# Linear attention, layer 1: keys summed with normalised rows over the tokens instead of with values, and another written order of its beginning

## The chip, the cores and the metric

One Trainium2 chip, one core. The metric is the device time of one execution in microseconds. Lower is better.

## The reference

Four layers run over x of 2048 tokens by 576 columns, bf16, in the order A, B, A, B:

```python
phi = lambda t: where(t > 0, t + 1, exp(t)) + 1e-6
def A(y, wqkv, wo):              # 32 heads of 18 columns
    q, k, v = split_heads(y @ wqkv)
    pq, pk = phi(q), phi(k)
    kv = einsum("bhsd,bhse->bhde", pk, v)      # sum over the tokens s
    z  = einsum("bhsd->bhd", pk)
    o  = einsum("bhqd,bhde->bhqe", pq, kv) / (einsum("bhqd,bhd->bhq", pq, z)[..., None] + 1e-6)
    return join_heads(o) @ wo
def B(y, w1, b1, w2, b2):        # 576 -> 4608 -> 576
    return gelu(y @ w1 + b1) @ w2 + b2
x = x + A(layernorm(x)); x = x + B(layernorm(x)); x = x + A(layernorm(x)); x = x + B(layernorm(x))
```

The layernorm has no weights, and both A layers use the same `wqkv` and `wo`, both B layers the same MLP weights. Since v = y @ wv, the sum over tokens of pk and v can be done in two ways: make v for each token and sum pk with v, or sum pk with y and multiply that sum by wv once.

## The kernel before

**Tiles.** The tokens are 16 tiles of 128 (t = 0 to 15). The 576 columns are five row blocks of 128 (`KD`, the last holds 64), the heads five groups (`G`: four of seven heads, 126 columns, and one of four, 72). Keys are worked on in two halves of 288 columns (`HALF`). `yT` holds the turned (transposed) normalised rows of all tokens, `wqkv_sb` the weights of query, key and value (column parts 0, 1, 2).

**Entry and rows.** `load_x0` and `load_wqkv` issue the loads on SyncE in a written order (`chained`): rows of tiles 0 and 1, all key weights, rows of tile 2, value weights, rows 3 to 5, query weights, the other rows. `LNPipe` normalises rows stage by stage, one stage per `tick`: statistics on VectorE, the reciprocal root as a power on GpSimd (L374), the normalisation (L391 on GpSimd for tiles 2 and from 4 on, L395 on VectorE) from the row tile into one of three buffers `y_ring`, five transposes on TensorE (L423), and a copy into `yT` (tiles 0 and 1 halved between ScalarE and VectorE, L426 and L427, later ones on ScalarE, L430). The core's own engine queues run in program order; `add_manual_dep(..., NOSYNC)` fixes the order of two instructions on one engine. A call of `pe()` chains TensorE's instructions in the order of the text.

**Layer 1, first part.** For each tile: `k_proj` (L542: two halves of five matmuls, each through phi into `pk`), the layernorm's step of a later tile, `v_proj` (L560 and L563: ten matmuls of 252 and 324 columns, copied into `v_ring` with a column of ones), `kv_acc` of the tile before (L584: five matmuls that sum pk with v and, through the ones, z into one PSUM accumulator), and, from tile 4 on, one of the 20 query blocks `q_proj` (L590: 126 rows by 512 tokens). `phi_from_psum` makes phi from two ScalarE passes (exp L467, copy L468) and two VectorE operations (L475, L479); `phi_by_dve` from the exp (L453) and two VectorE operations (L454, L456), the last of which reads PSUM. Masks for heads are built on GpSimd by `masks(n)`, some steps at each tile; the weights for the later stages are loaded by `late_pieces`, one piece at each tile from tile 3 on.

**Layer 3, first part** (`li > 0`) has another form already. `k_half` (L614) makes one half of the keys of a tile; `rows_by_keys` (L631), three steps behind, sums that half with the five row blocks of the tile's normalised rows: chunk 4 (64 columns and one of ones) into `k2_tail` in a bank of the pool `ps_h`, chunks 0 to 3 into two pairs of banks (`ps_acc`). It goes over all tiles with half 0 and then with half 1. `kv_groups` (L651) multiplies the sums `k2` by the value weights, 5 matmuls for each group, and masks the heads; `kv_wo_half` (L669) multiplies by `wo`; z comes from the column of ones (L695).

**Second part of both layers**: denominators (`den_stage`, `quad_stage`), scaling of the queries, and `wo_stage` (L824), which adds the residual and hands tiles to the layernorm of the MLP. The MLP's first matmul is L953.

**PSUM.** Pool `ps_h` has four banks, taken in turn by everything with the tag `h` (key halves, transposes, query blocks and others); `ps_acc` holds two pairs.

Of the kernel before, what the change touches and what calls it, by code (L numbers as in the profile page):

```python
# [15 lines left out]
P = 128  # L16
# [18 lines left out]
def build(tc, A_x, A_wqkv, A_wo, B_w1, B_b1, B_w2, B_b2, out, dbg=None, n_layers=4):  # L35
    nc = tc.nc
    dbg = dbg or {}
    with ExitStack() as ctx:
# [14 lines left out]
        pow_warm = const.tile([P, 1], F32, name="pow_warm")  # L53
        nc.gpsimd.memset(pow_warm[:], 1.0)
        nc.gpsimd.tensor_tensor(out=pow_warm[:], in0=pow_warm[:], in1=neg_half[:], op=ALU.pow)
# [5 lines left out]
        z_row = const.tile([P, 1], BF16, name="z_row")  # L61
# [9 lines left out]
        def inner_diag(tile_, lead, n):  # L71
# [7 lines left out]
            select(maskz[:], 1.0, ALU.not_equal, -126, [[0, 7], [0, DH]], 1),  # L79
            fill(z_row, 0.0),  # L80
            select(z_row[:], 1.0, ALU.not_equal, -126, [[0, 1]], 1),
# [62 lines left out]

        def load_x0(t):
            x0 = blk.tile([P, D], BF16, name="x0", tag="blk")
            chained(nc.sync.dma_start(out=x0[:], in_=x_in[t * P:(t + 1) * P, :]))
            x0_tiles[t] = x0

        def load_wqkv(part):  # L150
            cols = slice(part * D, (part + 1) * D)
            chained(nc.sync.dma_start(out=wqkv_sb[:, 0:4, cols],
                                      in_=A_wqkv[0:4 * P, cols].rearrange("(k p) n -> p k n", p=P)))
            chained(nc.sync.dma_start(out=wqkv_sb[0:64, 4, cols], in_=A_wqkv[4 * P:D, cols]))
# [4 lines left out]
        load_wqkv(1)  # L159
        load_x0(2)  # L160
        load_wqkv(2)
        load_x0(3)
        load_x0(4)
        load_x0(5)
# [3 lines left out]
        for i in (NY - 1, 0, 1):  # L168
            nc.vector.memset(y_ring[i][:], 0.0)
# [8 lines left out]
        for vr in v_ring:  # L178
            nc.gpsimd.memset(vr[:, 4, 72:126], 0.0)
            nc.gpsimd.memset(vr[:, :, 126:127], 1.0)  # L180
            nc.gpsimd.memset(vr[:, :, 127:128], 0.0)
# [29 lines left out]
        def bias_casts():  # L211
# [3 lines left out]
        late_pieces = [(lambda i=i: piece_w1(i)) for i in range(9)] + [piece_wo] + \  # L215
                      [(lambda i=i: piece_w2(i)) for i in range(6)] + [piece_b1_dma]
# [16 lines left out]
        def tail_ones():  # L233
            for c in range(NCB):
                nc.gpsimd.memset(tails(c)[:, :, 64:65], 1.0)
# [65 lines left out]
        class LNPipe:  # L301
# [11 lines left out]
            def tick(self, transposes=1):  # L313
                land()
                for it in list(self.items):
# [32 lines left out]
                    elif st == 0:  # L348
# [10 lines left out]
                        if it["kind"] == "A" and it["t"] == 1 and it["load"] is None and it["evac"] == "act":  # L359
                            tc.add_manual_dep(aggr.ins, dve_last["norm"], NOSYNC, reason="first rows first")  # L360
                        if it["kind"] == "A" and it["t"] == 2 and it["load"] is None and it["evac"] == "act":
                            tc.add_manual_dep(aggr.ins, dve_last["turned"], NOSYNC, reason="first rows first")
# [7 lines left out]
                        it["mv"], it["u"] = mv, u  # L370
                        dve_last["u"] = var_eps.ins.name
                    elif st == 1:
                        rstd = work.tile([P, 1], F32, name="ln_rstd", bufs=6)
                        nc.gpsimd.tensor_tensor(out=rstd[:], in0=it["u"][:], in1=neg_half[:], op=ALU.pow)  # L374
                        it["rstd"] = rstd
                    elif st == 2 and it["norm"] != "dve":
# [3 lines left out]
                        it["nmr"] = nmr  # L380
                    elif st in (2, 3):
# [12 lines left out]
                        else:  # L394
                            norm = nc.vector.tensor_scalar(out=y[:, 0:D], in0=xt[:, 0:D], scalar1=it["mv"][:, 0:1],  # L395
                                                           scalar2=it["rstd"][:, 0:1], op0=ALU.subtract, op1=ALU.mult)
                            if it["kind"] == "A" and it["t"] == 1 and it["load"] is None and it["evac"] == "act":
                                tc.add_manual_dep(norm.ins, dve_last["turned"], NOSYNC, reason="first rows first")
# [9 lines left out]
                    elif st == 4:  # L408
                        y = it["y"]
                        t = it["t"]  # L410
                        if it["evac"] == "dma":
                            turn_rows(y, t, it["kind"])
                            self.items.remove(it)
                            continue
                        tp = ps_h.tile([P, 512], F32, name="tp", tag="h")
                        tp = tp[:, 0:DPAD // 2].bitcast(BF16).rearrange("p (k n) -> p k n", k=KD)
                        first = it["kind"] == "A" and t < 2
                        tp2 = tp
                        if first:
                            tp2 = ps_h.tile([P, 512], F32, name="tp2", tag="h")  # L420
                            tp2 = tp2[:, 0:DPAD // 2].bitcast(BF16).rearrange("p (k n) -> p k n", k=KD)
                        for k in range(KD):
                            pe(nc.tensor.transpose(out=(tp if k < 3 else tp2)[:, k, :], in_=y[:, k * P:(k + 1) * P],  # L423
                                                   identity=ident[:]))
                        if first:
                            act_last["turned"] = nc.scalar.copy(out=yT[:, 0:3, t * P:(t + 1) * P], in_=tp[:, 0:3, :]).ins.name  # L426
                            copy = nc.vector.tensor_copy(out=yT[:, 3:KD, t * P:(t + 1) * P], in_=tp2[:, 3:KD, :])  # L427
                            dve_last["turned"] = copy.ins.name
                        elif it["evac"] == "act":
                            turned_tile = nc.scalar.copy(out=yT[:, :, t * P:(t + 1) * P], in_=tp)  # L430
                            if act_last["exp"] is not None:
# [11 lines left out]
        phi0 = {}  # L443
# [7 lines left out]
        def phi_by_dve(ps_ap, out_ap, rows, n):  # L451
            e = work.tile([P, 512], BF16, name="phi_e", bufs=3)
            act_last["exp"] = nc.scalar.activation(out=e[0:rows, 0:n], in_=ps_ap, func=ACT.Exp).ins.name  # L453
            nc.vector.tensor_scalar(out=e[0:rows, 0:n], in0=e[0:rows, 0:n], scalar1=1.0, scalar2=1e-6,  # L454
                                    op0=ALU.min, op1=ALU.add)
            top = nc.vector.scalar_tensor_tensor(out=out_ap, in0=ps_ap, scalar=C1, in1=e[0:rows, 0:n],  # L456
                                                 op0=ALU.add, op1=ALU.max)
            dve_last["phi"] = top.ins.name

        def phi_from_psum(ps_ap, out_ap, rows, n, turned_cols=False, after=None, dve_after=None, ident_after=None,  # L460
                          exp_first=False):
# [10 lines left out]
            if ident_after is not None:  # L472
                tc.add_manual_dep(ident_pass.ins, ident_after, NOSYNC, reason="first rows first")
# [3 lines left out]
            if ident_after is not None:  # L477
                tc.add_manual_dep(low.ins, dve_last["turned"], NOSYNC, reason="first rows first")
# [3 lines left out]
            dve_last["phi"] = top.ins.name  # L482

# [46 lines left out]
        def layer_A(li, next_kind, pre_a1=None):  # L530
            kvacc_of = {}
            pk_tiles = {}
            v_tiles = {}
            pq = {}

            def k_proj(t):
                tok = slice(t * P, (t + 1) * P)
                pk = blk.tile([P, D], BF16, name="pk", tag="blk")
                for half in range(2):
                    kp = ps_h.tile([P, 512], F32, name="k_ps", tag="h")  # L540
                    for k in range(KD):
                        pe(nc.tensor.matmul(kp[:, 0:HALF], lhsT=yT[:, k, tok],  # L542
                                         rhs=wqkv_sb[:, k, D + half * HALF: D + (half + 1) * HALF],
                                         start=(k == 0), stop=(k == KD - 1)))
                    phi = phi_by_dve if half == 1 and (li > 0 or t < 2) else phi_from_psum
                    if li == 0 and t == 0 and half == 0:
                        lnp.tick()
                        phi_from_psum(kp[:, 0:HALF], pk[:, 0:HALF], P, HALF, ident_after=act_last["turned"])
                        continue
                    phi(kp[:, 0:HALF], pk[:, half * HALF:(half + 1) * HALF], P, HALF)  # L550
                pk_tiles[t] = pk

            def v_proj(t):
                tok = slice(t * P, (t + 1) * P)
                va = v_ring[state["vcnt"] % NV]
                state["vcnt"] += 1
                begin = li == 0 and t < 2
                vp = ps_acc.tile([P, 2, 512], F32, name="v_ps", tag="accA" if begin and t == 1 else "accB")
                for k in range(KD):
                    pe(nc.tensor.matmul(vp[:, 0, 0:252], lhsT=yT[:, k, tok], rhs=wqkv_sb[:, k, 2 * D: 2 * D + 252],  # L560
                                     start=(k == 0), stop=(k == KD - 1)))
                for k in range(KD):
                    pe(nc.tensor.matmul(vp[:, 1, 0:324], lhsT=yT[:, k, tok], rhs=wqkv_sb[:, k, 2 * D + 252: 3 * D],  # L563
                                     start=(k == 0), stop=(k == KD - 1)))
                copy = nc.scalar.copy(out=va[:, 0:4, 0:126].rearrange("p (b g) c -> p b g c", b=2),
                                      in_=vp[:, :, 0:252].rearrange("p b (g c) -> p b g c", g=2))
                if begin:
                    for keys in ("exp", "phi"):
                        tc.add_manual_dep(copy.ins, act_last[keys], NOSYNC, reason="keys before values")
                if begin and t == 1:  # L570
# [475 lines left out]
        def pre_a1_layer0(t):  # L1046
# [6 lines left out]
            if t >= 4:  # L1053
                masks(2)
# [75 lines left out]
```

## Time and profile before

| | |
|---|---|
| Median of 3 runs | 764.03 us (763.88 to 764.38) |
| Profiled execution | 763.95 us, span 762.2 us |
| TensorE clock granted | 1.00 throughout |
| TensorE matmul busy | 756.4 us, 99% (6594 matmuls) |
| ScalarE / VectorE / GpSimd busy | 336.2 (44%) / 270.1 (35%) / 126.3 (17%) us |
| First key matmul of layer 1 | 7.02 us |
| z sums of layer 1 | about 70.3 us |
| First MLP matmul of layer 2 | 104.62 us |
| z sums of layer 3 | about 444 us |

A row of the timeline reads: start and duration in us (of a run of instructions, from the first's start to the last's end), engine (PE is TensorE's matmul, PEld its weight load, DVE VectorE, ACT ScalarE, POOL GpSimd, SPq the queue of SyncE), line, operation, output <- inputs, shapes, count, and in brackets the idle time before it and what ended that. Runs of pipelined matmuls overlap in this view, so a run's own duration is longer than the step to the next run. The chain of waits gives start, duration, engine, tile and line for each piece of the chain that ended last. The table of windows gives a stretch, its length, and each engine's busy time with its instructions.

### The profile page before, as it was taken

To read this page: it belongs to the slowest core of one execution; us is meant where nothing else is said; L and a number is where in the kernel's file an instruction comes from. 1 tells how busy PE (TensorE), PEld (TensorE's weight loads), DVE (VectorE), ACT (ScalarE), POOL (GpSimd) and SP (SyncE) were. 2 spreads that over 40 slices of the span, in tenths; PEclk is the share of its full clock that TensorE was granted. 3 is DMA by queue.
4 is the path that set the end of the run, shared out by engine and by line. 5 is a ranking of instruction groups with operands and counts; after the bars stand their busy time and mean duration, and the time that the engine had idled before them with its cause. 6 is when DMAs were issued, how large, how long until landed. Compare 5 with 4: busy or idle time off the path is not lost.

```text
span 762.2 us, 15786 instructions
## 1 busy us (share of the span) xinstructions
PE 756.4 (99%) x6594; PEld 491.0 (64%) x6594; DVE 270.1 (35%) x684; ACT 336.2 (44%) x750; POOL 126.3 (17%) x198
## 2 busy tenths in 40 slices
PE   8999999999999999999999999999999999999998
PEld 5777664675477457646777767447645754674476
DVE  7786963136023503400355678600240032000000
ACT  5888857204610750264056577560164037205600
POOL 4681241002000301200110005300020021001000
PEclk9999999999999999999999999999999999999999
DMA  8993483016402621330246007530231033011000
GB/s 245 257 326 53 157 281 82 16 49 181 106 25 73 180 75 45 99 80 9 71 125 208 1 26 236 207 83 16 72 88 48 16 126 82 9 32 56 1 9 24
DMA packets 80289, 73.82 MB, mean 97 GB/s; under 512 B 36698, under 2 KB 64858, under 8 KB 80218
## 3 DMA queue, kind: packets, MB, share of 16 engines
q1 hardware_dynamic: 80218, 72.82, 32.8%
q8 instruction: 51, 0.84, 0.5%
q14 instruction: 20, 0.16, 0.1%
HBM read 48.03 MB, written 24.77 MB: 96 GB/s over the span
## 4 chain that ended last, share of the span: by engine, by line
PE 98%; DMA 1%; DVE 0%; SPq 0%; issue 0%
PE m_ps L1011 36%; PE h_ps L953 20%; PE hp_ps L953 16%; PE q_ps L590 6%; PE wo_ps L824 5%; PE k_ps L542 3%; PE k_ps L614 3%; PE k_ps L631 2%; PE v_ps L563 1%; PE m_half L1011 1%; PE v_ps L560 1%; PE tp L423 1%; DMA wqkv_sb<-in_A_wqkv_dram 1%; PE kvacc L584 1%; PE k_tail L631 1%; PE rden_ps L788 0%
## 5 line engine op out<-in xcount | busy, mean ns | idle before, releaser
L1011 PE MATMUL m_ps<-w_sb,hT 128*128 128x288 bf16 x2232 | 274.8, 286 | 0.0
L1011 PEld LDWEIGHTS <-hT 128*128 128x128 bf16 x2304 | 224.8, 98 | 59.8 <-issue 3.4
L953 PEld LDWEIGHTS <-w_sb 64*128 64x128 bf16 x2304 | 124.5, 94 | 136.5 <-issue 1.9
L953 PE MATMUL hp_ps<-yT,w_sb 64*128 64x512 bf16 x1152 | 178.0, 376 | 0.0
L953 PE MATMUL h_ps<-yT,w_sb 64*128 64x512 bf16 x1152 | 147.9, 376 | 0.0
L958 ACT COPY relay_sb<-relay_sb 128x1 f32<-128x1 f32 x144 | 28.6, 199 | 259.7 <-PE h_ps L953 217.5
L949 ACT ACTIVATE hT<-h_ps,b1T 128x512 bf16<-128x512 f32 x144 | 91.3, 685 | 44.4 <-PE h_ps L953 44.4
L374 POOL TENSOR_TENSOR ln_rstd<-ln_u,neg_half 128x1 f32<-128x1 f32 x64 | 36.2, 567 | 403.1 <-DVE ln_u L365 225.7
L949 ACT ACTIVATE hT<-hp_ps,b1T 128x512 bf16<-128x512 f32 x144 | 91.3, 693 | 0.0
L520 DVE TENSOR_TENSOR xbf<-m_ps,xo 128x576 bf16<-128x576 f32 x15 | 11.4, 758 | 213.8 <-PE m_ps L1011 213.8
L520 DVE TENSOR_TENSOR xo<-m_ps,xo 128x576 f32<-128x576 f32 x16 | 12.1, 758 | 173.9 <-PE m_ps L1011 173.9
L503 POOL TENSOR_TENSOR xo<-xo,b_bc 128x576 f32<-128x576 f32 x32 | 40.9, 1283 | 101.4 <-DMA xo<-x_d 61.5
L953 PE MATMUL h_ps<-yT,w_tail 64*128 64x512 bf16 x144 | 54.1, 376 | 0.0
L953 PE MATMUL hp_ps<-yT,w_tail 64*128 64x512 bf16 x144 | 54.1, 376 | 0.0
L590 PE MATMUL q_ps<-yT,wqkv_sb 128*126 128x512 bf16 (+1 forms) x200 | 49.8, 381 | 0.0
L824 PE MATMUL wo_ps<-kvwo,pq 126*128 126x288 bf16 (+1 forms) x320 | 44.0, 286 | 0.0
L953 PEld LDWEIGHTS <-w_tail 64*128 64x128 bf16 x288 | 27.1, 94 | 17.1
L467 ACT ACTIVATE phi_e<-k_ps 128x288 bf16<-128x288 f32 x46 | 19.4, 421 | 38.8 <-PE k_ps L614 35.8
L824 PEld LDWEIGHTS <-pq 126*128 126x128 bf16 (+1 forms) x320 | 29.8, 97 | 9.7 <-DVE pq L793 0.4
L590 PEld LDWEIGHTS <-wqkv_sb 128*126 128x126 bf16 (+1 forms) x200 | 24.7, 131 | 11.7
L475 DVE TENSOR_SCALAR phi_e<-phi_e 128x288 bf16<-128x288 bf16 (+2 forms) x86 | 24.8, 288 | 19.9 <-ACT phi_e L467 19.1
L467 ACT ACTIVATE phi_e<-q_ps 126x512 bf16<-126x512 f32 (+1 forms) x40 | 23.9, 598 | 17.3 <-PE q_ps L590 17.3
(140 smaller groups left out, 654.9 us busy)
## 6 DMA issues: line engine op xcount, KB each, us to landing
xo<-x_d SPq DMA_DIRECT2D x48, 288.0 KB
x_d<-xo SPq DMA_DIRECT2D x32, 288.0 KB
xl<-x_d SPq DMA_DIRECT2D x24, 288.0 KB
y_d<-turned SPq DMA_DIRECT2D x40, 144.0 KB
w_sb<-in_B_w_dram SPq DMA_DIRECT2D x6, 864.0 KB
yT<-y_d SPq DMA_DIRECT2D x10, 512.0 KB
w_sb<-in_B_w_dram SPq DMA_DIRECT2D x9, 512.0 KB
x_d<-xn SPq DMA_DIRECT2D x16, 288.0 KB
```

The lines of the kernel that those rows point to most:

```text
L374: nc.gpsimd.tensor_tensor(out=rstd[:], in0=it["u"][:], in1=neg_half[:], op=ALU.pow)
L467: exp = nc.scalar.activation(out=e_out, in_=ps_ap, func=ACT.Exp)
L475: low = nc.vector.tensor_scalar(out=e[0:rows, 0:n], in0=e[0:rows, 0:n], scalar1=1.0, scalar2=1e-6, op0=ALU.min, op1=ALU.add)
L503: nc.gpsimd.tensor_tensor(out=xo[:], in0=xo[:], in1=b2_bc[:], op=ALU.add)
L520: total = nc.vector.tensor_tensor(out=xn[:, cols].rearrange("p (h n) -> p h n", h=2), in0=halves, in1=xo[:, cols].rearrange("p (h n) -> p ...
L590: pe(nc.tensor.matmul(qp[0:GR[g], :], lhsT=wqkv_sb[:, k, GO[g]:GO[g] + GR[g]], rhs=yT[:, k, c * CA:(c + 1) * CA], start=(k == 0), stop=(k ...
L631: pe(nc.tensor.matmul(dst, lhsT=lhsT, rhs=pk, start=(t == 0), stop=(t == NT - 1)))
L824: pe(nc.tensor.matmul(wp[:, half, 0:HALF], lhsT=pq[(g, c)][0:GR[g], j * P:(j + 1) * P], rhs=kvwo[g][0:GR[g], half * HALF:(half + 1) * HALF ...
L949: act_last["gelu"] = nc.scalar.activation(out=to, in_=ps, func=ACT.Gelu_apprx_tanh, bias=b1T[:, f:f + 1], scale=1.0).ins.name
L953: mm = pe(nc.tensor.matmul(dst[n], lhsT=wt, rhs=mv, start=(seen[n] == 0), stop=(seen[n] == 8)))
L958: relay = nc.scalar.copy(out=relay_sb[:, 1:2], in_=relay_sb[:, 0:1])
L1011: pe(nc.tensor.matmul(acc[half][:, 0:HALF], lhsT=hT[f][:, j * P:(j + 1) * P], rhs=w2_sb[:, f, half * HALF:(half + 1) * HALF], start=(f == ...
```

## The change

In layer 1 the values and their sums (`k_proj`, `v_proj`, `kv_acc`, `kv_from_sums`) go away, and both A layers use layer 3's functions. What differs in layer 1 is the order: keys of both halves of a tile are made together, half 0 is summed with rows in the same pass, and half 1 in a second pass over the kept keys and rows. `kv_groups` and `kv_wo_half` stand in that second pass, as in layer 3, and the second part of layer 1 takes layer 3's order.

```diff
-            for t in range(NT) if li == 0 else ():
-                ...
-                    k_proj(t)
-                ...
-                pre_a1(t)
-                v_proj(t)
-                if t >= (2 if li == 0 else 1):
-                    kv_acc(t - 1)
-                if t >= (4 if li == 0 else 2):
-                    q_proj(*q_left.pop(0))
+            if li == 0:
+                def keys(t):
+                    k_half(t, 0)
+                    k_half(t, 1)
+                ...
+                k_half(0, 0)
+                phi = k_half(0, 1, defer=True)
+                keys(1)
+                feed_and_tick(3, 2)
+                rows_by_keys(0, 0, (0, 1, 2, 3))
+                keys(2)
+                phi()
+                feed_and_tick(4, 2)
+                rows_by_keys(1, 0, (0, 1, 2, 3))
+                rows_by_keys(2, 0, (0, 1, 2, 3))
+                keys(3)
+                q_proj(*q_left.pop(0))
+                feed_and_tick(5, 1)
+                feed_and_tick(6, 2)
+                in_order("s0a s0b s1b g0 s1a g1 n0 n1 cd0 s2a s2b cd1 g2 u2 mi00 s3a ma00 n2 s3b mi10 cd2 g3 mi11 u3 ma11 "
+                         "s4b n3 mi20 ma10 ma20 s4a cd3 g4 u4 mi21 mi01 ma21 ma01 s5a s5b mi30 g5 ma30 u5 mi31 ma31")
+                in_order("ln0 re0 ln1 re1 ca0 ca1 e00 id00 e10 e11 ca2 id10 e20 e21 e01 ca3 e30 e31 id30 ca4")
+                rows_by_keys(3, 0, (0, 1, 2, 3))
+                for t in range(4):
+                    rows_by_keys(t, 0, (4,))
+                for t in range(4, NT):
+                    keys(t)
+                    pre_a1(t)
+                    if 4 < t < 13:
+                        masks(1)
+                    q_proj(*q_left.pop(0), defer=True)(after=act_last["turned"])
+                    lnp.tick()
+                    rows_by_keys(t, 0)
+                for _ in range(2):
+                    q_proj(*q_left.pop(0))
+            steps = [(t, 1) for t in range(NT)] if li == 0 else [(t, half) for half in range(2) for t in range(NT)]
+            ...
+                if li == 0:
+                    masks(2)
+                    rows_by_keys(t, 1)
+                    if t == 3:
+                        q_proj(*q_left.pop(0))
```

`in_order` writes down the order of the beginning on VectorE (first list) and ScalarE (second): s are statistics, g their sums, u and ln/re the variance and its reciprocal root, n a normalisation, cd and ca copies of turned rows, e, id, mi and ma the four steps of phi, with tile and half. The copy of tile 4's turned rows is the last on ScalarE's list, behind the first query block's two passes in the order of the text.

In `k_half` the first half of tiles 2, 6, 10 and 14 takes the route by VectorE as well:

```diff
-                    (phi_by_dve if half else phi_from_psum)(kp[:, 0:HALF], pk, P, HALF)
+                by_dve = half or li == 0 and t % 4 == 2
```

The rows of layer 1 stay on the chip: pairs of row tiles in the pool `rows` are normalised in place, columns 0 to 511 in the tile itself and the last 64, by GpSimd, into `v_ring` (`first_tail`), from where they are turned and summed. Tiles 2 and 3 are normalised by VectorE. The reciprocal root of tiles 0 and 1 is made on ScalarE:

```diff
+                        if "u" not in it:
+                            named(f"ln{it['t']}", nc.scalar.activation(out=rstd[:], in_=it["mv"][:, 1:2], func=ACT.Ln,
+                                                                       bias=eps_col[:, 0:1]))
+                            named(f"re{it['t']}", nc.scalar.activation(out=rstd[:], in_=rstd[:], func=ACT.Exp, scale=-0.5))
...
+                        if it["norm"] == "pool":
+                            for out, cols in ((xt[:, 0:4 * P], slice(0, 4 * P)), (tail, slice(4 * P, D))):
+                                norm = nc.gpsimd.tensor_scalar(out=out, in0=xt[:, cols], scalar1=it["rstd"][:, 0:1],
+                                                               scalar2=it["nmr"][:, 0:1], op0=ALU.mult, op1=ALU.add)
```

The loads come in another order, the key weights in two halves of 288 columns, the value weights last; of the late pieces, now one at each tile from tile 4 on, the output weights come fifth instead of tenth:

```diff
         load_x0(0)
         load_x0(1)
-        load_wqkv(1)
+        load_wqkv(1, 0)
         load_x0(2)
-        load_wqkv(2)
-        load_x0(3)
-        load_x0(4)
-        load_x0(5)
+        load_wqkv(1, 1)
+        for t in range(3, 6):
+            load_x0(t)
         load_wqkv(0)
         for t in range(6, NT):
             load_x0(t)
+        load_wqkv(2)
```

In the second part, layer 1 makes four query blocks after the z sums instead of six, and its head masks are built one step at a time at tiles 5 to 12 and two at a time in the second pass, instead of two at each tile from 4 on. One warm-up matmul stands between the transposes and the first keys instead of two. In the program as built TensorE has 56 matmuls fewer: 240 less for values and their sums, one warm-up less, 160 more for rows by keys, 25 more for the value weights.

## The prediction

> **What bounds the kernel now.** I read the page first: shares, then the chain that ended last.
>
> ```profile
> PE 756.4 (99%) x6594; PEld 491.0 (64%) x6594; DVE 270.1 (35%) x684; ACT 336.2 (44%) x750; POOL 126.3 (17%) x198
> PE 98%; DMA 1%; DVE 0%; SPq 0%; issue 0%
> ```
>
> TensorE is the bound throughout. A change can gain only by taking matmul time away or by an earlier first matmul, and loses whatever makes PE wait. Next the chain of waits over 0 to 140 us:
>
> ```profile
> 1.71 5.27 DMA wqkv_sb<-in_A_wqkv_dram
> 7.02 0.77 PE k_ps L542 x5
> ...
> 35.44 1.23 PE k_ps L542 x10
> 36.66 0.28 PE tp L423 x5
> 36.94 0.54 PE v_ps L560 x5
> 37.48 0.69 PE v_ps L563 x5
> 38.17 0.26 PE kvacc L584 x5
> ...
> 104.62 1.18 PE h_ps L953 x9
> ```
>
> PE begins at 7.02, when the key weights land, and the first MLP matmul is at 104.62. In between one token tile costs 1.23 (keys) + 0.28 + 0.54 + 0.69 + 0.26 = 3.00 us, and 1.10 for a block of queries. Busy time by stage, where layer 3 matters because it already does the new arithmetic (columns: stretch, its length and PE busy, then PEld, DVE, ACT, POOL, clock, DMA share, GB/s):
>
> ```profile
> 7.02:70.30 63.28, 63.28 (x549) 48.70 (x548) 47.13 (x164) 50.48 (x120) 37.42 (x67) 1.00 0.90 245
> 70.30:104.62 34.32, 34.32 (x364) 24.03 (x363) 28.62 (x67) 26.84 (x57) 10.10 (x18) 1.00 0.48 162
> 386.28:443.97 57.69, 57.69 (x416) 43.22 (x414) 35.34 (x109) 36.97 (x86) 2.26 (x4) 1.00 0.34 99
> 443.97:477.20 33.23, 33.10 (x364) 23.12 (x363) 27.38 (x63) 23.79 (x53) 10.68 (x18) 1.00 0.50 160
> ```
>
> Rows 1 and 2 are layer 1 up to the z sums and from there to the MLP, rows 3 and 4 the same of layer 3. PE has no idle time in either first part. The timeline of layer 3 gives the durations that follow:
>
> ```profile
> 410.38 0.78 PE L614 MATMUL k_ps<-wqkv_sb,yT 128*128 128x288 bf16 x5
> 411.19 0.41 ACT L467 ACTIVATE phi_e<-k_ps 128x288 bf16<-128x288 f32 x1 [0.51 <-PE k_ps L614]
> 411.50 0.41 ACT L468 ACTIVATE phi_a<-k_ps 128x288 bf16<-128x288 f32 x1
> 412.27 0.60 ACT L467 ACTIVATE phi_e<-q_ps 126x512 bf16<-126x512 f32 x1 [0.36 <-PE q_ps L590]
> 412.76 0.59 ACT L468 ACTIVATE phi_a<-q_ps 126x512 bf16<-126x512 f32 x1
> ...
> 428.18 0.41 ACT L453 ACTIVATE phi_e<-k_ps 128x288 bf16<-128x288 f32 x1
> 428.90 0.46 DVE L456 SCALAR_TENSOR_TENSOR pk<-k_ps,phi_e 128x288 bf16<-128x288 f32 x1
> ```
>
> A bank of keys is free when ACT's second pass is over, 411.50 + 0.41 - 410.38 = 1.53 after its first matmul; by DVE's route (exp on ACT, the rest on DVE) 428.90 + 0.46 - 428.18 = 1.18 after the exp starts, so 0.81 + 1.18 = 1.99.
>
> **The arithmetic, a gain.** Per tile the change removes 0.54 + 0.69 + 0.26 = 1.49 us of values and kvacc, 16 times: 23.84. It adds 10 matmuls of 288 columns (rows by keys) at the pace of the keys, 1.23, 16 times: 19.68; and the value weights applied once, 25 matmuls, 1.36 in layer 3. By counts: -2.80. By stages: 57.69 + 14 transposes of 0.28 (layer 3 gets its turned rows by DMA; those of tiles 0 and 1 lie before the first matmul, as now) = 61.6 against 63.28, and 33.23 against 34.32: -2.77. The MLP and layer 3 keep their work.
>
> **The entry, about nothing.** Key weights come in two halves with tile 2's rows between. The first half lets k(0,0) start at about 6.4, when tile 0's turned rows are there. The next matmuls need the second half, behind which as many bytes have landed (1,080 KB) as ahead of tile 2's rows now, at 7.55 in the trace: 7.6. Of what stood behind 7.02, 0.61 is then done: MLP at 7.6 + 61.6 + 33.23 - 0.61 = 101.8 against 104.62, -2.8. Half-width weight rows are 576 bytes a packet instead of 1,152. No row here prices that packet. The DMA view counts 891 packets (mean 1.07 KB) and 107.0% of 16 engines between 7 and 10 us, so 1.07 x 16 x 3 / 891 = 57.6 ns for one; between 53 and 60 us 5,855 (260 bytes) and 113.9%, so 21.8 ns. Linear between them, 576 bytes cost 36 ns, 1.17 times the time per byte of the large ones; the two halves, 648 KB at 316 GB/s, take 2.1 us, so 0.3 (bounds 0, and 2.1 if a packet took 57.6 ns whatever its size; taken by the interpolation, as 576 lies between the two rows). On SP's queue the second half takes the slots that the value weights have now (issues at 3.39 and 3.87); those go behind the last rows and are first used 45 us later, so their delay is covered, by 40 us of the first pass.
>
> **The banks, a loss.** ps_h has four banks. In layer 1 the tail sums (k2_tail) now hold one of them for the whole of both passes, so in each tile two key halves, the transposes and a query block take turns in three: the query block needs the bank of that tile's first keys. PE gets to it 0.615 + 0.615 + 0.28 = 1.51 after the tile's start; the bank is free at 1.53, with 0.05 for the signal 1.58: 0.07 lost, in 7 tiles. In tiles 6, 10 and 14 DVE's route sets it at 1.99 + 0.05 = 2.04: 0.53 each. Sum 0.5 + 1.6 = 2.1. Nothing covers it, as PE's queue is in order: transposes, sums and next keys stand behind that block. Layer 3 has no such case (its transposes need no bank), and before, values went to ps_acc.
>
> **Waits in the beginning, a loss.** At tiles 3 and 4 the copy of the next turned rows stands on ACT behind both passes of a query block. From that block's start S, ACT's passes end near S + 2.3 (exp at +1.2, 0.49 to the next, 0.59), the 128x640 copy takes 0.76: next keys at S + 3.05. PE has 1.10 + 0.28 + 0.615 = 2.0 in between at tile 4 (1.05 lost) and 0.36 more, sums of early tails, at tile 3 (0.69 lost). Tile 2's first keys take the bank of tile 1's, whose second pass stands behind a later exp and a copy in the written order: by those rows 0.57. Tile 3's normalised rows, late in DVE's written order, and the sums of tile 1: 0.35. Sum 1.05 + 0.69 + 0.57 + 0.35 = 2.7. No row of layer 1 shows these orders, so the bounds are wide: 0, if ACT and DVE reach the copies earlier than these durations in a row let them, and 4, if each copy meets one more pass of 0.41. I stay near the upper end, since an engine's queue is in order and the durations are this trace's.
>
> **POOL beside DVE, a small loss.** The norms of rows stay on POOL. Beside them:
>
> ```profile
> 33.08 0.95 POOL L391 TENSOR_SCALAR y_ring<-x,ln_rstd,ln_nmr 128x576 bf16<-128x576 bf16 x1
> 33.42 0.70 DVE L475 TENSOR_SCALAR phi_e<-phi_e 128x288 bf16<-128x288 bf16 x1
> ...
> 49.57 1.04 POOL L391 TENSOR_SCALAR y_ring<-x,ln_rstd,ln_nmr 128x576 bf16<-128x576 bf16 x1
> 49.77 0.23 DVE L475 TENSOR_SCALAR phi_e<-phi_e 128x288 bf16<-128x288 bf16 x1
> 50.11 0.66 DVE L479 TENSOR_TENSOR pk<-phi_a,phi_e 128x288 bf16<-128x288 bf16 x1
> ```
>
> A 0.23 us operation took 0.70 and ended with POOL's, at 34.1; once it ran untouched inside a norm and the next one paid. So a norm costs DVE some 0.35 to 0.47 once. Now that is hidden; after, it is seen where DVE frees a bank (tiles 6, 10, 14) or feeds early keys. One hit of 0.4 taken; bounds 0 and four hits, 1.8. The mask selects (1 to 2 us on POOL) move from two a tile to one, and two a tile in the second pass, where every key is ready; they are needed at the denominators some 10 us later: nothing, or 1 if they end late.
>
> The Trainium skill ("SBUF — State Buffer", section "SBUF: two separate sides") calls the port pair of DVE and GpSimd an exclusive lock: whichever starts first has it for its whole instruction and the other fully blocks. The trace agrees for the 0.70 row and not for the 0.23 row at 49.77. Taken alone, the rule puts each of the four hits on DVE's path, and the sum 1.4 higher.
>
> Edits with one answer: statistics of tiles 0 and 1 by ACT's Ln and Exp instead of POOL's power, rows in place, fewer memsets, the moved weight pieces, residual rows that wait for the row buffers of the second pass (free some 7 us ahead of their first use): off PE's path, nothing. What hides the last is the DMA queue's slack: the output weights, fifth instead of tenth, are used first in the second pass, and if that cover were gone the MLP would wait for its first weights, which the 104.62 row doesn't show now.
>
> **Sum.** -2.8 + 0.3 + 2.1 + 2.7 + 0.4 = +2.7, on the profiled execution's 763.95 (its span 762.2 and 1.75 around it, which the change doesn't touch): 766.6. The median of the runs shown, 764.03, is 0.1 from that execution, so nothing is corrected. About 0.2%, 1.5 us, is what a measurement of this kernel can tell: 762.5 to 765.5 is the same.
>
> **The rivals.**
> R1, faster, other side: ACT and DVE run ahead far enough that the early waits vanish, and the bank hand-over costs at most 1.2. What decides it is whether the bank is free before 1.51. For: 0.07 is small, and the exp sometimes starts earlier than 0.81. Against: 0.53 by DVE is no rounding. -2.8 to -1.6: 761.2 to 762.4.
> R2, same: only the bank waits and the packets come, not the early ones: -2.8 + 2.1 + 0.3 = -0.4, about 763.5.
> R3, slower still: every norm of POOL holds DVE, as in the 0.70 row: 1.4 more and some late mask selects, about 768. By the rule of the Trainium skill given above, this would be the outcome.
> That the change doesn't do what it says has no support: 56 matmuls fewer are issued.
>
> **How the numbers follow.** The forecast's own range is 765.0 to 768.0, chance 0.48 (0.40 slower, 0.08 within the band); R1 0.24 (0.22 faster, 0.02 same); R2 0.14, same; R3 0.14, slower. So faster 0.22, same 0.24, slower 0.54. The range runs from inside R1, 761.5, to inside R3, 768.6; some 0.15 is left out.
>
> **What would show it.** Right: first keys near 6.4 and a gap before the second; idle PE of 0.07, at tiles 6, 10 and 14 about 0.5, before q_ps; a gap near 1 us before the keys of tile 5; 33.2 us from the z sums to the MLP; first MLP matmul near 107. Wrong: no PE gaps in the first pass (R1, MLP near 102), a second part longer than 33.2 by late masks, or a later stage that moves.

## The result and the profile after

The changed kernel takes 768.88 us (median of 4, 767.88 to 769.74) against 763.95 (4 runs beside it): a ratio of 1.0064, 95% interval 1.0047 to 1.0082. It is slower, as forecast, but by 4.9 us instead of 2.7: 0.9 above the forecast's own range (765.0 to 768.0), and 0.3 above the wider one, which ends at 768.6. A second set of five runs on another occasion gave 767.95 (767.79 to 769.52), 1.0059 (1.0045 to 1.0073). Three of the nine executions lie at 769.5 to 769.7, with a mean granted clock of 0.997 or 0.998, the other six at 767.8 to 768.15; the profiled one (769.74, span 767.9) is of the three.

The profile after: the shares of its chain, and the chain of waits (start, duration, what):

```profile
PE 96%; DVE 2%; DMA 1%; ACT 1%; POOL 0%; issue 0%; SPq 0%; DVEq 0%; POOLq 0%
```

```profile
3.40 4.24 DMA wqkv_sb<-in_A_wqkv_dram
7.68 2.03 PE k_ps L601 x15
...
52.32 0.60 ACT phi_e L511
52.95 1.29 DVE phi_e L517
54.35 0.63 DVE pq L519
54.98 0.94 DVE phi_e L496
55.94 0.47 DVE pk L498
56.45 2.29 PE q_ps L578 x5
...
110.06 1.18 PE h_ps L953 x9
```

Before, nothing but TensorE stood between the key weights and the MLP. Now pieces of ScalarE and GpSimd stand in the chain in the beginning, and four operations of VectorE at tile 14, and the MLP starts at 110.06 instead of 104.62: 5.44 of the 5.7 us by which the span grew. The windows, cut at the end of the z sums, show that the first part is to blame. The second takes 32.74; with the z sums, which start at 76.85, it is 33.21, the 33.23 of layer 3 as forecast:

```profile
6.39:77.32 70.93, 65.76 (x492) 48.23 (x492) 50.95 (x163) 43.71 (x99) 39.72 (x73) 0.98 0.79 223
77.32:110.06 32.74, 32.60 (x359) 22.74 (x360) 26.65 (x63) 23.20 (x51) 10.08 (x18) 1.00 0.52 170
```

TensorE's waits from its first key matmul up to the MLP, from the view of waits; before, the same view had one line, ahead of the first keys:

```profile
PE k_ps L542 <- DMA wqkv_sb<-in_A_wqkv_dram: 0.7, 1, 0.7
```

Now it has five:

```profile
PE q_ps L578 <- DVE pk L498: 2.8, 3, 2.1
PE k_ps L601 <- DVE ln_u L381: 0.9, 1, 0.9
PE k_ps L601 <- DMA wqkv_sb<-in_A_wqkv_dram: 0.5, 1, 0.5
PE tp L464 <- POOL x L410: 0.4, 1, 0.4
PE k_ps L601 <- ACT phi_a L512: 0.4, 1, 0.4
```

Columns are the total, how many, the longest. These count from the end of the last matmul, which lies 0.16 after the next could start (a run of five keys is recorded with 0.78, and the next run starts 0.615 on), so 0.9 is a loss of 1.03, 0.4 one of 0.57. The 0.9 wait is put down to ln_u, but the timeline has the copy of tile 5's turned rows ending at 22.37, just ahead of the keys at 22.42. At tile 4 the transposes (L464) waited for GpSimd's normalisation, which stood behind a fill; TensorE reached that tile's keys at 18.19, after the copy had ended at 18.10:

```profile
15.23 0.52 POOL L583 MEMSET pq<- 32x512 bf16 x1
15.85 0.77 POOL L410 TENSOR_SCALAR x<-x,ln_rstd,ln_nmr 128x512 bf16<-128x512 bf16 x1
16.68 0.40 PE L464 MATMUL tp<-ident,x 128*128 128x128 bf16 x4 [0.44 <-POOL x L410]
17.41 0.69 ACT L469 COPY yT<-tp 128x640 bf16<-128x640 bf16 x1
18.19 1.39 PE L601 MATMUL k_ps<-wqkv_sb,yT 128*128 128x288 bf16 x10
...
21.67 0.70 ACT L469 COPY yT<-tp 128x640 bf16<-128x640 bf16 x1
22.42 1.40 PE L601 MATMUL k_ps<-wqkv_sb,yT 128*128 128x288 bf16 x10 [0.87 <-DVE ln_u L381]
```

What stands beside tile 14, on GpSimd and VectorE, in the timeline (SELECT builds a mask, MEMSET is a fill):

```profile
52.86 0.64 POOL L66 TENSOR_SCALAR_AFFINE_SELECT quad_mask<-quad_mask 128x512 bf16<-128x512 bf16 x1
52.95 1.27 DVE L517 TENSOR_SCALAR phi_e<-phi_e 126x512 bf16<-126x512 bf16 x1 [0.70 <-ACT phi_e L511]
53.44 0.64 POOL L70 MEMSET head_bc<- 128x640 bf16 x1
54.02 0.69 POOL L66 TENSOR_SCALAR_AFFINE_SELECT quad_mask<-quad_mask 128x512 bf16<-128x512 bf16 x1
54.35 0.63 DVE L519 TENSOR_TENSOR pq<-phi_a,phi_e 126x512 bf16<-126x512 bf16 x1
54.66 3.23 POOL L66 TENSOR_SCALAR_AFFINE_SELECT head_bc<-head_bc 128x630 bf16<-128x630 bf16 x3
54.91 1.00 DVE L496 TENSOR_SCALAR phi_e<-phi_e 128x288 bf16<-128x288 bf16 x1
55.94 0.46 DVE L498 SCALAR_TENSOR_TENSOR pk<-k_ps,phi_e 128x288 bf16<-128x288 f32 x1
```

The mask steps written in the second pass run here, 12 us before that pass begins (64.89): GpSimd's queue had nothing left in front of them after the last normalisation (norm), and nothing ties them to the pass. Beside them VectorE's operations take 1.27, 0.63 and 1.00 us, where the same ones take 0.29, 0.42 and 0.23 elsewhere; the one that reads PSUM keeps its 0.46. The bank that the next query block needs is free when the last of these ends, at 56.40, and TensorE is idle from 54.40 to 56.45.

By tile the loss falls so (start of the first keys of tile t minus the work between, at 0.615 for keys or sums, 0.28 for transposes, 1.10 for a query block, hence 3.225 for a full tile):

| stretch | length | work | lost |
|---|---|---|---|
| second key half (7.68) to keys of tile 5 (22.42) | 14.74 | 11.92 | 2.82 |
| tile 5 to tile 14 (52.73), nine tiles | 30.31 | 29.03 | 1.28 |
| tile 14 to tile 15 (59.74) | 7.01 | 3.225 | 3.79 |
| tile 15 to the z sums (76.85) | 17.11 | 17.15 | 0 |

At tile 14 the loss has two parts. The wait is 2.2. The rest, 1.6, is pace: the granted clock reads 0.50 from 56.5 to 59.5, and the query block takes 2.29 instead of 1.24. In the profile of the second set the same wait is there and the clock stays at 1.00; then tile 14 takes 5.41, 1.6 less. One line of each, the first set's first:

```profile
56.45 2.29 PE L578 MATMUL q_ps<-yT,wqkv_sb 128*126 128x512 bf16 x5 [2.05 <-DVE pk L498]
```

```profile
56.27 1.24 PE L578 MATMUL q_ps<-yT,wqkv_sb 128*126 128x512 bf16 x5 [2.06 <-DVE pk L498]
```

The Trainium skill ("TensorE: Matmul & The Clock Gate", section "Part 1: The HAM clock gate") has the gate at half pace after an idle window of about 3.4 us, and calls it variable from run to run. Half pace and the variation agree; the idle time here was 2.05 us, shorter than that window.

### The profile page after: what moved, and what is told of

It is laid out like the page before. It is cut to its first block, busy times and chain, and to the rows that moved or that the text cites. A ratio compares the mean times of both kernels' runs of the same rounds, so it can differ in the third digit from the quotient of the medians.

```text
span 767.9 us, 15683 instructions
## 1 busy us (share of the span) xinstructions
PE 757.9 (99%) x6538; PEld 489.7 (64%) x6538; DVE 272.5 (35%) x675; ACT 326.2 (42%) x726; POOL 129.5 (17%) x203
## 4 chain that ended last, share of the span: by engine, by line
PE 96%; DVE 2%; DMA 1%; ACT 1%; POOL 0%; issue 0%; SPq 0%; DVEq 0%; POOLq 0%
PE m_ps L1011 36%; PE h_ps L953 20%; PE hp_ps L953 16%; PE q_ps L578 6%; PE wo_ps L834 5%; PE k_ps L601 5%; PE k_ps L626 4%; PE m_half L1011 1%; PE k_tail L626 1%; PE tp L464 1%; DMA wqkv_sb<-in_A_wqkv_dram 1%; PE rden_ps L798 0%; PE kv_ps L650 0%; PE den_ps L771 0%; DVE pq L824 0%
## 5 line engine op out<-in xcount | busy, mean ns | idle before, releaser
L601 PE MATMUL k_ps<-wqkv_sb,yT 128*128 128x288 bf16 x320 | 46.8, 286 | 1.8 <-DVE ln_u L381 0.9
L601 PEld LDWEIGHTS <-yT 128*128 128x128 bf16 x320 | 31.1, 98 | 10.6 <-ACT yT L469 1.2
```

Of the source, the lines that this page charges most:

```text
L601: pe(nc.tensor.matmul(kp[:, 0:HALF], lhsT=yT[:, k, t * P:(t + 1) * P], rhs=wqkv_sb[:, k, D + half * HALF: D + (half + 1) * HALF], start=(k ...
```

## The experiments

All are the changed kernel with one edit (e6, e7 and e8: several moves together), five or six runs each, eleven of e8, beside the kernel before (medians 763.96 to 764.05). The starts of some steps in their profiles, in us; for the MLP it is its first matmul (104.55 in the kernel before, 109.99 in the profile above, each 0.07 ahead of the chain's row):

| kernel | keys of tile 2 | tile 5 | tile 14 | tile 15 | z sums | MLP | median time (range) |
|---|---|---|---|---|---|---|---|
| after, second set | 10.70 | 22.24 | 52.55 | 57.96 | 75.00 | 108.13 | 767.95 (767.79-769.52) |
| e1_masks_late | 10.89 | 22.45 | 52.75 | 56.48 | 75.38 | 108.52 | 768.41 (767.67-768.75) |
| e2_fill | 11.09 | 22.65 | 52.95 | 58.38 | 75.41 | 108.54 | 767.90 (767.62-768.20) |
| e3_no_dve14 | 11.05 | 22.61 | 52.91 | 57.85 | 74.88 | 108.01 | 767.80 (767.36-767.87) |
| e4_sums_behind | 12.38 | 23.93 | 53.99 | 58.24 | 76.28 | 109.42 | 768.15 (767.34-769.48) |
| e6_masks_after_fill | 10.68 | 22.23 | 52.54 | 56.26 | 73.30 | 106.44 | 766.25 (765.87-767.38) |
| e7_begin | 10.98 | 21.24 | 51.55 | 56.96 | 74.00 | 107.13 | 767.28 (766.96-768.31) |
| e8_all | 10.77 | 21.02 | 50.41 | 53.68 | 70.71 | 103.84 | 763.94 (763.41-765.86) |
| f1_masks_spread | 10.52 | 22.06 | 54.44 | 58.25 | 75.28 | 108.42 | 768.36 (768.08-769.18) |
| f2_keys_whole | 11.95 | 23.51 | 53.81 | 59.24 | 76.27 | 109.40 | 769.10 (768.20-771.63) |

**e5_after_again** is the changed kernel itself, with which the others are compared.

> The changed kernel itself once more, as the standard of these runs on the same chip: 768.9 (767.9 to 769.7 in its first runs). If the half-pace stretch after tile 14's wait comes in every execution, the runs keep within 0.5 us of one another; if not, they spread by 1.5.

The runs spread by 1.7, so the half pace comes only in some executions. From here on the first row is the comparison; the expectations of e1 to e4, e6 and e8 were worked out from the profile with the half pace, whose tile 14 is 1.6 too high.

**e1_masks_late**: in the second pass,

```diff
+                if after is not None:
+                    tc.add_manual_dep(inst, after, SYNC, reason="masks behind the last keys")
...
-                    masks(2)
+                    masks(2, after=last_keys)
```

> The changed kernel, with the mask selects of its second pass made to wait for the last keys' phi; the same selects run, later. Theory (the selects reach GpSimd's queue early, run at 53 to 59 us and hold VectorE while tile 14 needs it for a bank): tile 14's query block waits 0.5 us instead of 2.2, the clock stays at 1.0, so 3.2 us less than the changed kernel, about 765.7. Rival (the hand-over by VectorE is itself the wait, whatever GpSimd does): at most 0.5 us less.

Tile 14 does what the theory says: 52.75 to 56.48 is 3.73, the same as tiles 6 and 10. The time doesn't follow (768.41). The selects ran at 63.05 to 69.1, and behind them in GpSimd's queue was the fill that the second pass's query block needs:

```profile
69.17 0.52 POOL L586 MEMSET pq<- 32x512 bf16 x1
69.73 0.43 DVE L522 TENSOR_TENSOR pq<-phi_a,phi_e 126x512 bf16<-126x512 bf16 x1 [3.52 <-POOL pq L586]
70.07 0.41 DVE L659 TENSOR_TENSOR kvT<-kv_ps,maskz 126x252 bf16<-126x252 f32 x1
70.54 0.34 PE L671 MATMUL kvwo_half<-wo_sb,kvT 126*126 126x288 bf16 x1 [1.66 <-DVE kvT L659]
```

VectorE waited 3.52 for the fill, kvT stood behind it, and TensorE lost 1.8 there. So the prediction's "nothing, or 1 if they end late" was wrong in both places where the selects were tried.

**e6_masks_after_fill** adds one order, the fill ahead of the selects:

```diff
+                    tc.add_manual_dep(inst, pool_last["pq"], NOSYNC, reason="masks behind the last fill")
```

> As e1_masks_late, with one thing mended: GpSimd's fill of the second pass's query block (pq, L586) goes ahead of the selects in GpSimd's queue, since there VectorE, and kvT behind it, waited 3.5 us for that fill. Theory (selects running at 53 to 59 us cost 3.3, and the 1.66 before kvwo_half in e1 was the fill's place in the queue): no wait before kvwo_half, 3.3 less than the changed kernel, first MLP matmul at 106.7, about 765.5. Rival (the selects cost VectorE as much wherever they run, so kvT is late all the same): 1.0 to 1.5 left before kvwo_half, about 766.8.

No wait is left before kvwo_half, tile 14 takes 3.72, and the z sums come 1.70 earlier, as does the median time (766.25 against 767.95). Of the 3.3 forecast, 1.6 was the half pace, which most runs don't have. VectorE at tile 14 without the selects:

```profile
52.76 0.29 DVE L521 TENSOR_SCALAR phi_e<-phi_e 126x512 bf16<-126x512 bf16 x1 [0.70 <-ACT phi_e L515]
53.30 0.42 DVE L523 TENSOR_TENSOR pq<-phi_a,phi_e 126x512 bf16<-126x512 bf16 x1 [0.25 <-ACT phi_a L516]
53.79 0.23 DVE L500 TENSOR_SCALAR phi_e<-phi_e 128x288 bf16<-128x288 bf16 x1
54.06 0.46 DVE L502 SCALAR_TENSOR_TENSOR pk<-k_ps,phi_e 128x288 bf16<-128x288 f32 x1
```

This settles who held VectorE: the same operations at the same place, 0.29, 0.42 and 0.23 again. The lock of the Trainium skill ("SBUF — State Buffer", section "SBUF: two separate sides") agrees with these two sets of rows. The rule has the loser wait for one instruction of the winner; the operation of 1.27 took about as long as a select and a fill of 0.64 each, so it was not let in between them.

**e2_fill**: nine matmuls on zeros ahead of the last transposes.

> The changed kernel, with nine extra matmuls on zeros (512 columns, into the transposes' own bank) ahead of the last transposes at tile 14: TensorE is as late with that tile's query block but not idle before it. Theory (of the 3.75 us lost at tile 14, 2.2 are the wait and 1.55 the clock granted after the idle time): 1.55 us less, about 767.3, with the clock at 1.0 over 56 to 60 us. Rival (the slow records come from what VectorE, GpSimd or the DMA do then): no change.

Tile 14 takes 5.43 with the fill and 5.41 without it where the clock stays up. None of its five runs has a mean clock under 1.0; of the changed kernel's nine, three have 0.997 or 0.998. The kernels with a wait of 2.05 to 2.07 at tile 14 (the changed one, e7, f2) have such a clock in five of 20 runs, those whose waits are 1.75 or less in none of 41. So the half pace goes with the long wait; e2 is the only one that takes away the idle time alone, and its five runs are too few to show that by themselves. The expected gain of 1.55 doesn't come, as the runs compared with (767.95) mostly have no half pace to lose.

**e3_no_dve14**: `by_dve = half or li == 0 and t in (2, 6, 10)`.

> The changed kernel, with the first key half of tile 14 through ScalarE's two passes, as in its neighbours, instead of by VectorE; tiles 2, 6 and 10 keep VectorE's route. The selects still run beside it. Theory: the query block of tile 14 gets its bank from ScalarE, so its 2.2 us and the clock's 1.55 go; the second half, still by VectorE and held, frees the bank of the next keys late, by up to 1 us: 2.5 to 3.7 us less, about 765.8. Rival (any work of VectorE held by the selects stops TensorE there, by a shifted place): under 1 us less.

The query block no longer waits (it starts at 54.48, 1.57 after the tile), but the sums of the tile do, for keys that VectorE finishes late beside the selects, and a loss of 1.7 comes in place of 2.2:

```profile
57.24 0.28 PE L626 MATMUL k_tail<-pk,v_ring 128*65 128x288 bf16 x1 [1.52 <-DVE pk L519]
```

The rival had it: tile 14 takes 4.94 instead of 5.41, and the medians differ by 0.15. The place that I named (the next tile's bank) was the wrong one.

**f1_masks_spread**: `masks(2)` at tiles 5 to 12 in place of `masks(1)`.

> The changed kernel, with two mask steps at each of tiles 5 to 12 instead of one, so that none is left for the second pass and each tile's steps stand between two norms on GpSimd. Theory (a hold costs TensorE only where VectorE frees a bank: tiles 6 and 10, and 14): no selects run at tile 14, which falls from 2.2 to 0.5; tile 10, now beside a fill or a select of quad_mask or head_bc, waits up to 1 us more: 1 to 2.5 us less than the changed kernel, about 766.3. Rival (a select costs the same wherever it runs): no change.

No gain, 768.36. Tile 14 takes 3.81, but tile 10 takes 5.11, tile 9 3.68 and tile 12 3.53. At tile 10 VectorE is held by the fill and the first select of head_bc while it should free a bank:

```profile
40.07 0.64 POOL L70 MEMSET head_bc<- 128x640 bf16 x1
40.13 0.72 DVE L517 TENSOR_SCALAR phi_e<-phi_e 126x512 bf16<-126x512 bf16 x1
40.78 0.97 POOL L66 TENSOR_SCALAR_AFFINE_SELECT head_bc<-head_bc 128x630 bf16<-128x630 bf16 x1
40.95 1.04 DVE L519 TENSOR_TENSOR pq<-phi_a,phi_e 126x512 bf16<-126x512 bf16 x1
...
42.69 1.24 PE L578 MATMUL q_ps<-yT,wqkv_sb 128*126 128x512 bf16 x5 [1.75 <-DVE pk L498]
```

The holds cost most where they meet a tile whose bank VectorE frees; here it was tile 10. In tiles 9 and 12 another wait costs 0.4 and 0.3: TensorE's sums wait for keys that VectorE finishes late. At tile 9 it had waited 1.11 for a fill behind two selects, as in e1.

**e4_sums_behind**: in the first pass `rows_by_keys(t - 1, 0)` ahead of the query block in place of `rows_by_keys(t, 0)` behind it.

> The changed kernel, with the sums of the tile before put ahead of each tile's query block in the first pass, so the block asks for its bank 0.61 us later; same matmuls. Theory of the banks (0.47 us at tiles 6 and 10, 0.035 at eight others, 2.2 at tile 14): those of 0.47 and 0.035 go, 1.2 us, and tile 14's falls by 0.6: 1.8 us less, about 767.1. Rival (the pace of 3.26 us a tile and the waits at 6 and 10 have another cause): no change.

Tiles 6 and 10 take 3.52 instead of 3.72, the others 3.30 instead of 3.265: over tiles 5 to 13 30.06 instead of 30.31. The wait moved to the next use of a bank: the transposes now start 0.10 late in each tile, and the blocks of tiles 6 and 10 still wait 0.22. The gain of 1.2 that I expected from the banks came to 0.25. Only tile 14 gained more (4.25 instead of 5.41). But from tile 15 to the z sums it takes 18.04 instead of 17.04. The sums of tile 4, taken out from ahead of tile 5's keys, leave 0.61 of idle time there, as those keys come no earlier, and are paid for at the end, with 0.40 for keys that come late for the sums. So 0.4 is left of the 1.4, and the median, 768.15, shows no gain. The profile's starts carry 1.7 more, all of it ahead of tile 2's keys: the first 20 key matmuls, from 7.50, took 3.70 us, where e1's took 2.61. The first ten start 0.24 apart instead of 0.12, with a clock read as 1.00; what slowed them stays open.

**e7_begin**: copies of tiles 4 and 5 ahead of the query blocks' passes, the first fill early.

```diff
-                q_proj(*q_left.pop(0))
+                phi = q_proj(*q_left.pop(0), defer=True)
                 feed_and_tick(5, 1)
                 feed_and_tick(6, 2)
+                phi(after=act_last["turned"])
```

> The changed kernel, with three moves in the beginning: at tiles 3 and 4 the copy of the next turned rows goes ahead of the query block's two passes on ScalarE, and GpSimd's fill of the first query block is done before tile 4's norm is due. Theory (at tiles 4 and 5 TensorE waits 0.6 and 1.03 for these): keys of tile 4 0.6 earlier, those of tile 5 1.0 earlier in all, as the second half then waits 0.45 for a bank; 1.0 less than the changed kernel. Rival (the beginning is VectorE's: busy 12.6 of the 14.5 us from 6.4 to 20.9): less than 0.3.

Keys of tile 2 to keys of tile 5 take 10.26 instead of 11.54, 1.3 less; the median falls by 0.67. So the early waits hang on these moves, 0.6 of it ahead of tile 4's keys and 0.7 ahead of tile 5's; the copy and the fill were moved together, so how much each gave isn't told apart. Part of the gain isn't seen at the end: from the MLP's first matmul on this profile takes 658.3, the second set's 657.8, and why stays open.

**f2_keys_whole**: `load_wqkv(1)` and then tile 2's rows.

> The changed kernel, with the key weights loaded whole ahead of tile 2's rows, as before the change. Theory (the second half of the weights lands at 7.6 either way or a little earlier, and tile 2's rows, 0.4 us later, are needed by 8): first keys at about 7.0, the same keys of tile 2 within 0.3, no change in time. Rival (the 576-byte packets of the halves cost 0.3 or more): 0.3 to 1 us less.

Both were wrong: it is slower, 769.10. The first keys start at 7.23, but the statistics of tile 2 at 7.93 instead of 6.60, and with them its keys at 11.95, 1.25 later. So the beginning hangs on tile 2's rows; no cost of the narrower packets shows.

**e8_all**: e6 and e7, VectorE's route for first halves at tile 2 only, and tile 0's sums ahead of tile 1's statistics.

```diff
-                by_dve = half or li == 0 and t % 4 == 2
+                by_dve = half or li == 0 and t == 2
```

> e6 and e7 together, and of the first halves only tile 2's by VectorE (tiles 6, 10 and 14 by ScalarE), and VectorE's sums of tile 0 no longer written behind the statistics of tile 1. Theory (matmuls -2.8; lost: beginning 2.8, banks 1.3, tile 14 3.75): takes back 1.0 + 0.9 + 3.75 of it, first MLP matmul at about 104.5, 763.4, the same as the kernel before within its noise. Rival (what is mended turns up as other waits, as in e1): 765 or more.

763.94, ratio 1.0001 (0.9992 to 1.0009): the whole loss is taken back, and no more. Every tile from 5 on takes 3.26 to 3.28, and the view of waits up to the MLP has two lines left:

```profile
PE k_ps L609 <- ACT phi_a L516: 0.4, 1, 0.4
PE k_ps L609 <- ACT yT L473: 0.2, 1, 0.2
```

The MLP's first matmul is 0.7 ahead of that of the kernel before, but from there to the end this profile takes 0.9 longer (658.56 against 657.65); one wait of 0.42 for the row sums ahead of the last MLP (at 478.15) is part of it, the rest is open.

## Why the prediction was right and wrong

| term | forecast | measured |
|---|---|---|
| MLP without the new waits | 101.8 | 109.99 - 2.82 - 1.28 - 3.79 - 0.08 = 102.0 |
| entry, beyond 7.6 | 0.3 | 0.08 |
| waits in the beginning | 2.7 | 2.82 |
| banks, tiles 5 to 13 | 1.55 | 1.28 |
| tile 14, hold and pace | 0.53 + 0.4 | 3.79, or 2.19 without the half pace |

- The arithmetic held: in e8 the second key half starts at 7.58, as forecast, and the MLP at 103.84; less 1.52 and 0.41 lost up to tiles 5 and 15 that is 101.9.
- The beginning held in its sum and in three of its four parts: 0.58 ahead of tile 2's keys (forecast 0.57; the bank and the last copy of that tile's rows come within 0.01 of each other), 0.40 at tile 3 (0.35), 1.01 at tile 5 (1.05). At tile 4 the number, 0.83 (0.69), is luck: the forecast had TensorE wait for the copy behind the query block's passes, and it waited for GpSimd's norm behind a fill, which has no term.
- The banks held at tiles 6 and 10: 0.47 a tile over their neighbours, against 0.53, and 0.035 against 0.07. But e4 shows that the query block's place isn't the whole of it: asked for later, the wait moves on.
- The entry's 7.6 was right, and no run shows the 0.3 for narrower packets: 0.08 in this profile, nothing in e8. What follows hangs on tile 2's rows more than on the key weights (f2).
- **The step that failed** is that of GpSimd beside VectorE: the mask selects "move from two a tile to one, and two a tile in the second pass, where every key is ready". Their place in the text is not a time. GpSimd had nothing to wait for and ran them at 52.86 to 58.9, beside tile 14, which was in the forecast with 0.53 for VectorE's route and one hit of 0.4 for the whole kernel. It was four operations in a row, 2.2 of wait where 0.9 was forecast; e6 takes back 1.7 by putting the selects behind the last keys and the fill, f1 gives it back at tiles 9, 10 and 12. The half pace after it, 1.6 in three of nine executions, had no term at all. Without it, as in the median of the second set (767.95), the time lies just inside the forecast's range; that would be luck, since this step is wrong all the same.
- The rival with the lock (R3, about 768) came nearest in time. Its mechanism is the one shown, its place isn't: not every norm holds VectorE at cost, one run of selects does. R1 and R2 fall, since all the early waits came.

## What to carry to other kernels

An instruction that waits for nothing runs when its engine's queue reaches it, whatever stage it is written in; for each step moved on a queue that runs ahead, ask when it will start and what the other engines do then. Price what is held by the tightest place that it can reach, not by the mean: here VectorE's time was free in nearly every tile, and dear in the three where it hands over the next query block's bank; held for long, it also made keys late for their sums (e3, f1). A wait that is taken away is gone only if the next use of the same bank, or the next instruction in the same queue, has room, as e1, e3 and e4 show.

## What was not expected of the hardware

After 2.05 us without matmuls the granted clock fell to 0.50 for some 3 us in one profile and not in another with the same wait, 1.6 us of time in one tile. And a VectorE operation of 0.29 us took 1.27, through two operations of GpSimd that followed each other without a gap, one of them a fill.
